# A cubic on VectorE factored so that GpSimd makes half of it, with a new order and more tiles on VectorE

## The chip, the cores and the metric

The kernel runs on one core of a Trainium2 chip. The metric is the device time of one execution in microseconds (us). The engines that matter here are TensorE (PE, with its weight loads PEld), ScalarE (ACT), VectorE (DVE) and GpSimd (POOL); transfers are issued from SyncE's queue (SP).

## The reference

Four layers in a row, with the weights of set A, B, A, B; each adds attention to the layer's input x of 2048 rows of 512, in float32:

```python
def _A_ref(x, wq, wk, wv, wo):          # _B_ref is the same
    B, S, D = x.shape                   # 1, 2048, 512
    H = 32
    Dh = D // H                         # 16
    q = (lambda x, *d: x.transpose(*d))((x @ wq).reshape(B, S, H, Dh), 0, 2, 1, 3)
    k = x @ wk
    v = x @ wv
    scores = jnp.einsum("bhqd,bkd->bhqk", q, k) * (Dh ** -0.5)
    p = _softmax(scores, axis=-1)
    o = jnp.einsum("bhqk,bkd->bhqd", p, v)
    return (lambda x, *d: x.transpose(*d))(o, 0, 2, 1, 3).reshape(B, S, H * Dh) @ wo
...
x = A_x
x = x + _A_ref(_layernorm(x, axis=-1), A_wq, A_wk, A_wv, A_wo)
x = x + _B_ref(_layernorm(x, axis=-1), B_wq, B_wk, B_wv, B_wo)
...                                     # A and B once more
```

One key head and one value head serve all 32 query heads. The scores are 4 layers x 32 heads x 2048 x 2048, which makes 4096 tiles of 128 partitions x 1024 columns, and every one of these numbers has to go through an exponential.

## The kernel before

The work is a sequence of pairs (layer, block of 512 queries, group of heads). For a score tile TensorE multiplies 64 keys by the queries (operands `kop` and `qt`), an engine takes the exponential into a slot of `pt` in SBUF (16 slots of 128x1024 float32, `NPT`), and TensorE multiplies that by the values (`vop`) into the accumulators `acc`.

There are two ways to the exponential. Most tiles go to one of two PSUM buffers `st` and ScalarE takes their exponential in one instruction (`score`, L813, letter S of the order). The others, 440 of the 4096, go in two halves through one PSUM bank, `by_v`, and VectorE makes the exponential itself (`exp_first` and the chain that it adds): two instructions of 512 columns scale the scores out of PSUM so that their integer bits are an exponent and a fraction (L845, letter I), and five instructions over the 1024 columns in SBUF then finish the tile: the fraction as a number between 1 and 2 (`mant`, L859), the power of two (L861), and a cubic in `mant` by Horner's rule, in three instructions that each have two inputs in SBUF (L862, L863 and L856). A tile's chain has two scratch buffers, `mant` and `poly`, and there are two sets of them, so that at most two chains are under way; the letters 0 and 1 of the order take the next instruction of the older and the younger one.

Beside this, TensorE makes the next layer's queries, keys and values and the last layer's output rows in the bank `beside`; VectorE empties that bank, sums and divides (letters X, G, D), and a one-column copy `seen` (L941, letter Y) lets it tell TensorE how far it may count. GpSimd squares the queries and keys for a range check (`sq` L476, `ksq` L452) and raises the variances to the power -1/2 (`rstd` L412).

What sets the order is a string written out in the program, `ORDER`: one letter for each step, and each engine's queue is filled in that order. Nothing is reordered later; each engine takes its own queue in order and waits for semaphores. A tile for VectorE is taken 24 half tiles ahead of ScalarE's (`AHEAD`).

Of the kernel before, what the change touches and what calls it, by code (L numbers as in the profile page):

```python
# [50 lines left out]
C0, C1, C2 = 7.247527122497559, 6.331161975860596, 0.5959731936454773  # L51
# [11 lines left out]
    "0SFSXaaXSsqGqS0qclSqIlqqSGlqqqrSYlmId0pSpml0Smp0ppmSppm0pSddpS0aaSQlmYeSXmlSXmalXSXFXSlmXaXXXSXgGpSGpmdI"
    "pSppmrYSqIcl0qSql0mSql0qeSqlm0SqalS0malSolSQmYppmpSppmdSXalXSmlmpSppmSsYGclIqSoqGrSIem0rSqlq0qSqe0lmSlmI"
    "Slm0aSpm0ppSpsmppISb0dSQlXmlS0maXSa0lqSql0qqSqlqlq0SqrmlSmGqqSIclSYmpppsSpGppImS0ppmpS0pmd0pSalS0mlmSQlX"
    "mlSXma0SqelqSoeSqlqqlqSrYmpSpmppIpsSIbm0prSd0bSGlS0lmaSGpmSIma0lSslmSIe0mlSQqlmXSa0aSXlm0SF0SlmlXXmS0iqS"
    "elIoS0qclSoqGSqrXaXSlXmIaSGlSXbb0S0pmppSQXpmXlmS0pmlSpmXdlXSmXlSalmSrdSXImaXlSXaS0lmcSGqloSGoqS0qelsSYIm"
    "ap0Sb0pSmp0pdSQpml0SddpSDDa0aSdlSYqqlmlXSslXmSeIeqSqrlqSqqlqqI0Sqa0lGSmqSDlmlqGSlSDDlma0SppmpSQ0dppmSpm0"
    "ppSddpXSlmlXSmaDDpSgYqqSqlqIrqSqIcl0Smr0lmSl0mSpmpIlmSGpslSGbdISa0aSslm1lSQ0qqlSqql0mlSImaS0alSDpmpmDpSD"
    "pdrSDDmlImlXSslS1maXlGSFXSaSGbd0SalS1ma0Sqelq0SqqlqSqeDlqDqSDcSIlma0SaS0bbSpmDDrpSIdd0pSgXmlSXmlS0qa0lqS"  # L70
    "qqlq0SqlmlSIqlqqS0lmaSYrpImpSpm0ppsSbIml0Spm0pSmal0SdlSd0aSrmlISpm0lsSm0al0SaSlqIme0SqlmSXalSXma0pSpdpSD"
    "mppDpmSDrmlISmg0lSqIqcS0c0eSrqqlqISql0mSfa1Sa0lSpmlm0Sp0mlSbImpSQa0lSml0sSqlmlSXmlImSgXlm0SqcISl0qqlq0So"
    "eSGmfS0alSIpmppSGpn1mS0pmprSma0l0SpmlSmIlpm0SpmlSm0apSsaIlSm0lsSlImql0Sqql0mSalXSmlXmrSIlmS0rFSXmaSDDp0d"
    "lSpm0lmSIpmlXSpmbSalSXXm0lmS0qelqS0qqlqSc0lqSscSIlmXlmS0rmlISpm0dpS0lmkSdIlS0mllsSm1aS0lmlSm0aSIa0lSrqml"
    "ISmg0Salm1Slm0SlmaIS0arS0mlmSlImlS0faS0aaSQlImS0asl0SmlImSg1lmGSmSGllS0maS1lm0lSmaSXalSm0aSlmXSIalm0SrmS"
    "ImaXlSmlS0rmlSXmaS0lSIlmmXSlsSIlmXmlSXrmlSmlXSlmmSlSXXmal0S1PPS0PP0SPPP0SPPS0PPSPS0aXa0SppmpSpmIdp0Sppsp"
    "mSIppmpS0salS0ma0Sc0eSoeISc0lqSqqreISmlXrmS1cl1qSql1mSqlml0SqlmS0aeSqIemS0lmlsSImlS0ppmg0SpmIbS0pbSpm0pm"
    "pSQprmSIlm0aSsa0SqeIeS0mlSXXlmXmrSIlmgX0SlmSXmaSGlGSXm1lS0almS0lmSlmXmlS0mlSX0malSImlSXlmDmlSXDmlXDSa0lm"
    "SrmlISmgXS1FXSXalmDDXSlmXSF0SlmXaSXlmSXXF0SXalmXSlm0SFISaXaSXlmS0PPPS0PPPSfDlSIma0SrlmDSDPPPDDS0PPIPSXml"
    "SXmal0SFSXmaXlXSmlXsSXXlXmXIeS0qqerSma1l1SolS0malSIqlqq0Saa0SaSpmp0pdSsppdISppmDkS0pmplmDDSQlmSIa0aS0qlq"  # L80
    "qSaXlSmXaS0pmpppSb0dSpmlSYqqrqeSIlq0mrSGloqlGSmmS0cIlSm0aSlm0lSmnpsSDDpmIa0SsalS0mlSIqa0rSIqlmlXSrmXaS0a"
    "eSq1qloS0elmS1qaS0lmeSIqcS0aaS0lmSppm0ppmSppsdISppm0psSpmIlmS0lmp0SlmmrSIlml1SqrmXlSmXaS0clqS1qce0SqqlSI"
    "mal0SmlS0pmpbSppmDpS0ddpSdDlDsSpmlImS0glmISa0rSqIqlqS0salSXma1lSmXaS0FSXmlSQ0qclqS0qlm0SlqmlS0meSqcIlS0m"
    "aSlqYrmSIpdp0pSrm0dpS0dnSmlGlSppmGSIpma0lSgSImlm1lSrm1qlSXmaS1lqqe0SolqSa0aSaISpm0nspSbImpS0lmrS0ma0lSqq"
    "eSIlm0eSqlqsSDDlIma0SlmS0dpsp0pSpmXaSa0eSolImSc0lSma0SlmrSIpmpd0pSsl0mpSIpmdp0SlmlS0mlmSqe0eSqlorISmeS0f"
    "a0SaIlSm0ppmpSdXlSml0qeSqc0SqalDSqeYsSlImb0Sppm0pSmp0pdSsa0lSQpmdSIal0SrmlmISlq0qqrSqa0lSIma0SlslmISppm0"
    "SlmfSGllSGmmSXXaDlSDmlmXSlm1lSXm1aSXa1lSmlmXS0lmlSXma0SalSXIma0SlmlSDDsIlmSmgXlS0maXISl0mrSXImal0SrmlS1m"
    "aXS1al0SFSXmlXSlmXaXSF0SlSXaXaSXXFISlmXSXaa0SFSXslmSIlmXlsS0mppmpSp1bS0bmpSp0bmS0lmlS0malSqqlIqS0qeqrScI"
    "eS0qiSIemXlSmXar0SFISmgXl0SmlmSQXlXmlSmX0aSlmXlXSX0maSlImlSX0maGSrSIgGlS0maDSlDmlDSml0mSlmlS1ma0Slml0Sml"
# [180 lines left out]
def fast_path(ctx, tc, x_in, weights, out, flag):  # L270
# [26 lines left out]
    def masks():  # L297
# [4 lines left out]
        with nc.allow_low_precision("zeros and ones"):  # L302
# [1090 lines left out]
```

## Time and profile before

| | |
|---|---|
| median of 3 runs | 3446.65 us (3446.0 to 3450.4) |
| the profiled execution | 3446.91 us, its span 3445.1 us |
| busy, share of the span: PE | 3371.2 us, 98% |
| ACT | 3389.2 us, 98%, 3686 instructions |
| DVE | 3267.9 us, 95%, 4420 instructions |
| POOL | 133.5 us, 4%, 137 instructions |
| granted TensorE clock | 0.998 |

The busy time of PE is modelled from pipelined matmuls; that of ACT and DVE comes from their own records. A DVE record begins a little before its predecessor's ends, so that the step from one start to the next tells more of what an instruction takes of the engine than its duration does.

### The profile page before, as it was taken

The page shows a single profiled execution, that of the slowest core. Times are in us where ns is not written, and L with a number is a line of the kernel's source. Part 1 is how long each engine was busy: PE and PEld are TensorE (multiplying, and loading weights), DVE is VectorE, ACT ScalarE, POOL GpSimd, SP SyncE. Part 2 cuts the span into 40 slices and gives each one's busy share as a digit, 9 for nine tenths or more (in the row PEclk, how much of TensorE's full clock was granted, in tenths as well). Part 3 has the DMA queues.
Part 4 walks back from the last instruction along what each step waited for, and adds up shares of the span by engine and source line. Part 5 has one row for each costly group of instructions (what it writes and reads, how often), then busy time and mean ns, then how long its engine had stood idle before and what let it go on. Part 6 is the DMA issues. An engine that isn't in the chain of part 4 may idle for free.

```text
span 3445.1 us, 206723 instructions
## 1 busy us (share of the span) xinstructions
PE 3371.2 (98%) x97983; PEld 2102.8 (61%) x97983; DVE 3267.9 (95%) x4420; ACT 3389.2 (98%) x3686; POOL 133.5 (4%) x137
## 2 busy tenths in 40 slices
PE   9999999999999999999999999999999999999998
PEld 5666666555566666656566666665656666565554
DVE  7889999999989999999998999999999899999998
ACT  8999999999999999999999999999999999999998
POOL 3000000000000000000000000000000000000000
PEclk9999999999999999999999999999999999999999
DMA  3221111010012111101002211110101211110010
GB/s 102 69 80 46 35 46 49 25 44 26 27 47 65 44 44 43 40 25 50 19 30 58 54 53 37 38 50 15 50 19 50 59 41 37 39 49 26 27 38 21
DMA packets 93826, 147.81 MB, mean 43 GB/s; under 512 B 30056, under 2 KB 47976, under 8 KB 92968
## 3 DMA queue, kind: packets, MB, share of 16 engines
q1 hardware_dynamic: 91400, 133.64, 13.2%
q8 instruction: 767, 12.57, 1.5%
q10 hardware_dynamic: 1568, 0.85, 0.1%
q14 instruction: 91, 0.75, 0.1%
HBM read 90.57 MB, written 34.59 MB: 36 GB/s over the span
## 4 chain that ended last, share of the span: by engine, by line
PE 58%; ACT 28%; DVE 8%; issue 2%; DMA 1%; SPq 0%; DVEq 0%; ACTq 0%
PE acc L531 31%; ACT pt L813 28%; PE st L531 15%; PE beside L531 9%; PE by_v L531 2%; DVE pt L845 1%; DVE poly L862 1%; DVE poly L863 1%; PE beside L425 1%; DVE pt L856 1%; DVE mant L859 1%; PE beside L568 1%; DMA qt<-qs 1%; DVE pt L861 1%; DMA rec<-rs 0%
## 5 line engine op out<-in xcount | busy, mean ns | idle before, releaser
L813 ACT ACTIVATE pt<-st 128x1024 f32<-128x1024 f32 x3656 | 3374.9, 1083 | 28.5 <-PE st L531 23.8
L531 PE MATMUL acc<-pt,vop 64*32 64x256 f32 (+1 forms) x52088 | 2904.6, 432 | 5.3 <-issue 2.0
L531 PE MATMUL st<-qt,kop 64*32 64x512 f16 x29248 | 1784.8, 380 | 44.4 <-ACT pt L813 28.9
L531 PEld LDWEIGHTS acc<-pt,vop 64*32 64x32 f32 x52088 | 1341.9, 106 | 273.5 <-DVE sum L960 15.0
L531 PEld LDWEIGHTS <-kop 64*32 64x32 f16 x32768 | 799.2, 90 | 904.4 <-issue 620.0
L845 DVE TENSOR_SCALAR pt<-by_v 128x512 int32<-128x512 f32 x880 | 601.8, 684 | 54.7 <-PE by_v L531 40.1
L863 DVE SCALAR_TENSOR_TENSOR poly<-poly,mant 128x1024 f32<-128x1024 f32 x440 | 538.7, 1225 | 3.8
L856 DVE SCALAR_TENSOR_TENSOR pt<-poly,pt 128x1024 f32<-128x1024 f32 x440 | 537.3, 1222 | 4.0
L862 DVE SCALAR_TENSOR_TENSOR poly<-mant 128x1024 f32<-128x1024 f32 x440 | 537.4, 1222 | 0.0
L531 PE MATMUL beside<-xnT,wq 64*32 64x512 f16 x5760 | 432.0, 376 | 1.0 <-DVE qs L480 0.4
L531 PE MATMUL beside<-wo,ot 64*32 64x512 f16 x5376 | 390.4, 376 | 1.2 <-DVE xt L500 1.1
L531 PE MATMUL by_v<-qt,kop 64*32 64x512 f16 x3520 | 352.3, 378 | 7.9 <-DVE pt L845 4.6
L859 DVE TENSOR_SCALAR mant<-pt 128x1024 int32<-128x1024 int32 x440 | 302.1, 687 | 13.6
L861 DVE TENSOR_SCALAR pt<-pt 128x1024 int32<-128x1024 int32 x440 | 303.6, 690 | 3.7
L531 PEld LDWEIGHTS <-wq 64*32 64x32 f16 x5760 | 167.7, 92 | 46.6 <-issue 10.5
L531 PEld LDWEIGHTS <-ot 64*32 64x32 f16 x5376 | 153.9, 92 | 40.7 <-issue 5.2
L476 POOL TENSOR_TENSOR sq<-qs 128x512 bf16<-128x512 f16 x64 | 75.4, 1178 | 885.1 <-DVE qs L473 867.9
L531 PE MATMUL beside<-xnT,wkv 64*32 64x512 f16 x1344 | 97.1, 376 | 1.2 <-issue 1.2
L960 DVE COPY sum<-acc 128x512 f32<-128x512 f32 x126 | 83.8, 685 | 8.9 <-PE acc L531 6.3
L412 POOL TENSOR_TENSOR rstd<-var,nhalf 128x4 f32<-128x4 f32 x15 | 23.5, 1566 | 1428.7 <-DVE var L411 1428.7
L473 DVE TENSOR_SCALAR qs<-beside 128x512 f16<-128x512 f32 x62 | 42.4, 684 | 11.2 <-PE beside L531 4.6
L500 DVE SCALAR_TENSOR_TENSOR xt<-beside,xt 128x512 f32<-128x512 f32 x61 | 42.0, 688 | 6.1 <-PE beside L531 4.0
(124 smaller groups left out, 802.6 us busy)
## 6 DMA issues: line engine op xcount, KB each, us to landing
qt<-qs SPq DMA_DIRECT2D x85, 512.0 KB
qs<-qs SPq DMA_DIRECT2D x127, 128.0 KB
rec<-rs SPq DMA_DIRECT2D x63, 256.0 KB
xs<-xt SPq DMA_DIRECT2D x48, 256.0 KB
xt<-xs SPq DMA_DIRECT2D x48, 256.0 KB
sum<-sum SPq DMA_DIRECT2D x252, 32.0 KB
xt<-in_A_x_dram SPq DMA_DIRECT2D x30, 256.0 KB
out_dram<-xt SPq DMA_DIRECT2D x15, 256.0 KB
```

Of the source, the lines that this page charges most:

```text
L473: V.tensor_scalar(qs[:, 0], ps, BIG, -BIG, ALU.min, ALU.max)
L476: G.tensor_tensor(sq, qs[:, 0], qs[:, 0], ALU.mult)
L500: V.scalar_tensor_tensor(x, ps, 1 / VS / WS, x, ALU.mult, ALU.add)
L531: PE.matmul(o[32 * j:32 * j + 32], w[j][h], x[j][h], start=start, stop=stop, skip_group_check=True, tile_position=(64 * r, 32 * j))
L813: e = A.activation(pts[:, i], st[s], AF.Exp, scale=SCALE / UP / UP).ins
L845: w = V.tensor_scalar(e[:, 512 * r:512 * r + 512], by_v, SCALE / UP / UP * LOG2E * 2.0 ** 23, LEAD, ALU.mult, ALU.add).ins
L856: writer[i] = V.scalar_tensor_tensor(p, poly, C0, p, ALU.add, ALU.mult).ins
L859: lambda: V.tensor_scalar(mant.bitcast(I32), e, 0x3FFFFF, 0x3F800000, ALU.bitwise_and, ALU.bitwise_or),
L861: lambda: V.tensor_scalar(e, e, 0x7FC00000, HALVES, ALU.bitwise_and, ALU.bitwise_or),
L862: lambda: V.scalar_tensor_tensor(poly, mant, C2, mant, ALU.add, ALU.mult),
L863: lambda: V.scalar_tensor_tensor(poly, poly, C1, mant, ALU.add, ALU.mult),
L960: V.tensor_copy(sums[pr, odd], acc[odd])
```

## The change

The cubic is written as (m + r)(m(m + b) + c), with r `ROOT`, b `SLOPE` and c `REST`. Right behind the write of `mant`, GpSimd makes `poly` in two instructions over 128x1024 float32 in SBUF: m + b (b read from a 128x1 tile, broadcast along the row), and that times m. VectorE keeps two of its three instructions of the cubic, p = (m + r) p, which needs nothing from GpSimd, and p = (poly + c) p, which waits for GpSimd's second. The order string is replaced by another, with 508 tiles on VectorE and 3588 on ScalarE (before 440 and 3656).

```diff
-C0, C1, C2 = 7.247527122497559, 6.331161975860596, 0.5959731936454773
+ROOT, SLOPE, REST = 1.0617902024664836, -0.4658170088210063, 6.825761911968984
...
+    slope = one.tile([P, 1], F32, name="slope")
+    V.memset(slope, SLOPE)
...
+        def first():
+            V.tensor_scalar(mant.bitcast(I32), e, 0x3FFFFF, 0x3F800000, ALU.bitwise_and,
+                            ALU.bitwise_or)
+            G.tensor_tensor(poly, mant, slope.to_broadcast([P, 1024]), ALU.add)
+            G.tensor_tensor(poly, poly, mant, ALU.mult)
+
         def last():
-            writer[i] = V.scalar_tensor_tensor(p, poly, C0, p, ALU.add, ALU.mult).ins
+            writer[i] = V.scalar_tensor_tensor(p, poly, REST, p, ALU.add, ALU.mult).ins
 
         chains.append(deque([
-            lambda: V.tensor_scalar(mant.bitcast(I32), e, 0x3FFFFF, 0x3F800000, ALU.bitwise_and,
-                                    ALU.bitwise_or),
+            first,
             lambda: V.tensor_scalar(e, e, 0x7FC00000, HALVES, ALU.bitwise_and, ALU.bitwise_or),
-            lambda: V.scalar_tensor_tensor(poly, mant, C2, mant, ALU.add, ALU.mult),
-            lambda: V.scalar_tensor_tensor(poly, poly, C1, mant, ALU.add, ALU.mult),
+            lambda: V.scalar_tensor_tensor(p, mant, ROOT, p, ALU.add, ALU.mult),
             last]))
```

In the order string the letters for TensorE's steps around S are other too; 62 letters Y (`seen`) become 229, and 84 letters P (a product over the whole array at once) become 60, the rest being done in steps of the half arrays. The letters X, D, F, G and Q are as many as before.

In VectorE's queue, some four tenths of the way through, the tiles stand one behind another before (`pt<-by_v` are the two halves of a tile, `mant` opens the chain, and `pt<-poly` closes it; the numbers tell buffers apart):

```order
L845 TENSOR_SCALAR pt<-by_v 128x512
L859 TENSOR_SCALAR mant_38253<-pt 128x1024
L861 TENSOR_SCALAR pt<-pt 128x1024
L862 SCALAR_TENSOR_TENSOR poly_38254<-mant_38253 128x1024
L845 TENSOR_SCALAR pt<-by_v 128x512
L863 SCALAR_TENSOR_TENSOR poly_38254<-poly_38254,mant_38253 128x1024
L845 TENSOR_SCALAR pt<-by_v 128x512
L856 SCALAR_TENSOR_TENSOR pt<-poly_38254,pt 128x1024
L859 TENSOR_SCALAR mant_38378<-pt 128x1024
```

In the changed queue the lines have moved (L847 the halves, L858 `mant`, L868 the power of two, L869 the factor m + r, L864 the closing product):

```order
L847 TENSOR_SCALAR pt<-by_v 128x512
L858 TENSOR_SCALAR mant_39159<-pt 128x1024
L864 SCALAR_TENSOR_TENSOR pt<-poly_39043,pt 128x1024
L868 TENSOR_SCALAR pt<-pt 128x1024
L847 TENSOR_SCALAR pt<-by_v 128x512
L869 SCALAR_TENSOR_TENSOR pt<-mant_39159,pt 128x1024
L847 TENSOR_SCALAR pt<-by_v 128x512
L858 TENSOR_SCALAR mant_39264<-pt 128x1024
L864 SCALAR_TENSOR_TENSOR pt<-poly_39160,pt 128x1024
```

A tile is closed behind the opening of the next one now, one Horner instruction is gone, and between `mant` and the closing product of a tile stands a whole period of the queue.

GpSimd's queue before, in the first layer, holds the range check and the variances alone:

```order
L412 TENSOR_TENSOR rstd<-var,nhalf 128x4
L452 TENSOR_TENSOR ksq<-kop_2_99 128x512
L412 TENSOR_TENSOR rstd<-var,nhalf 128x4
L452 TENSOR_TENSOR ksq<-kop_3_100 128x512
L476 TENSOR_TENSOR sq<-qs 128x512 x12
```

In the changed kernel, at the same place (L454 `ksq`, L478 `sq`):

```order
L860 TENSOR_TENSOR poly_2978<-mant_2977,slope 128x1024
L861 TENSOR_TENSOR poly_2978<-poly_2978,mant_2977 128x1024
L454 TENSOR_TENSOR ksq<-kop_3_102 128x512
L860 TENSOR_TENSOR poly_3300<-mant_3299,slope 128x1024
L861 TENSOR_TENSOR poly_3300<-poly_3300,mant_3299 128x1024
L478 TENSOR_TENSOR sq<-qs 128x512
L860 TENSOR_TENSOR poly_3683<-mant_3682,slope 128x1024
L861 TENSOR_TENSOR poly_3683<-poly_3683,mant_3682 128x1024
```

The pairs `poly` (1016 instructions in all) have come between the others.

More of the change, by code (lines that the diff above doesn't have):

```diff
@@ L63 @@
[L63 to L77, printed above, removed]
@@ L228 @@
[L228 to L230 removed]
+    "QXPPPPPPPPSSPPPPSXlXmSPPSPPSPPPPSrSPPPPSIsXlmSIaXaS0lmS0F0SaaXSlmXSaXXaSQXlmXSlmXXlmSXaX0SalSGSXaXgSGFIS"
+    "XlmrSXmaXlSIFS0lmXSaXaSXXF0SXmalXSml0SQFSXaaXSlm0qSqleSYGmdnSsIpmnSpmlSYGrqqlIqqSqel0qS0mlqS0lmeSmaYpSpm"
@@ new lines @@
+    "ppSmplXmSlmXSQXlmXmlXSFSXXaX0aSaXaXXSmSGfXlISGlslSImaXrSXaXSXlmXmSXaX0lSm0mSIlmlXsSXFISaXSQXlmaXS1F1SaXS"
+    "aXlmSXXFGSfXlSGlS0aaXSlm0SFSXlmlImSXlmS0bbS0pspmpSQbIpSmYe0lqS0qlo0ScqlSqqlqqSgYIlmSpdGrSmIlmgXSXlmSGFlS"
+    "0maSXlXmlSXmlmXS0aXlXSXXmXaSQ0lmXlISmXlmS0alSmXGfSIaXaSXsSGlmXaXXS0mSaIlmXSrmSXF0SXaa0SXalmXS0FSQaXSlmXl"
+    "mXXSF0SaXSaXaSGFGSlSIlmXfSXae0SqlIoS0lqql0qSqseSIqclSmY1pd1Sppmp0SQbdp0SpmnSmXalXSmlXSXmlXFSrmXXlXSXXmIa"
+    "pGSpppSGps0pmpSppmIpmSppmYl0Sqqc0Sc0eSqcSqlqXlmSQaXSlmdpSp0mppSmpppmSppmpSmkYlqSIlqqlqSqqrqlSqIqeS0lq0ml"
@@ new lines @@
+    "SGmmSGelSXmaXSlm0pSdpb0SQpmnSpmdpSYlmlqSqqlqSlqqlqqSrqlqSqqIlYmSpmlSXaXlsSImpppmS0pmp0dSpGlS0nmaSGpmppSm"
+    "YelqSQqqeS0lqqeSqYlmSqYalqSqlmSlmgSXXImaSrIFSXXma0Spp0mppSpm0aSppmlSYXqGqlqSGmmSXeXlqXqSQe0mSqlmlSYXbXmp"
+    "SdXlXSmaXlSmlSrqqlmXSIqegSmYplSIXma0SaXlSGoqqS0lqmGlSoeS0lmaSQYppmSppmpmS0ppmlSYqqlmSYpYmeSqglSYbImpSdXl"
+    "SmaXrSIceSmY0lS0pmbGSlpSGpmd0pSalSQYmppmSY0clqSqlqDDqSqlqlYmSppmpSYmeXrSmalISmXgSeImlSY0bd0Sdl0SmllSGnSD"
+    "pmGdpSDaDlSQ0mlmpSpmDDlYSqqYalSqqlqSqYlmlSqrmlSYIpmgYSqlImlqS0mg0SaIaGSrqqSIaXaSGllS0maS1lmlXSQmg1Sm0alS"
@@ new lines @@
+    "FISXma0rSppmpSIpmppm0rSpmlS0pmIaSDpmlS0pmlGSpspmDlGSmSDmaIlSq0qeSeq1jSa0aSqlIqSlm0a0SlqqsSlImlm1Slqq1Slm"
+    "XaSXrmlmS0ppmpSpImplm0SppspmSIpml0SsalSImd0pSa0lS0mlmrSqlIoS1qcl1Smrql1SmaSa0lSmlImSDDpslYmISqe1eSf1aS0q"
+    "lqSaXaXSaSIpmp0pkSmppmIpSd0lSsa0lSbImS0a0lSmlmSDqlqeDSDqrqlqISml0qSfaSIe0lmS0lmqSQ0lqmlSslImSc1lmS1lmrS1"
+    "malSd0dSlmlXSmXlmSGpmpIpSpppGsSIppmp0mSglmISppm0pSm0al0SmlSroIlqqSqc1lS1mrql1SmalS0qlmSlmIlqSDDqlsqSIaXa"
+    "S1lmSXa1gSm0aSFISXmar0SalSImaXrSmlSmalS1a0SlmlmXXS0lmSIa0aSlsmISlmXls1Sma0SalSDmlDmlDSmlS0bIbSXpmdpSp0bS"
@@ new lines @@
+    "pmpmXrSlImlS0faS0qc0Sqlq0lqSqqeSXqeeSmIaSXlsIlmSlr0mSlmISQlm0lsSImlm0Ssa0lSmlDDS1maSGmlXSmlSGla0Sa0SaIaX"
+    "SrmlISml0mrSa1Sa0aSmSIlm0lsSImlm0rSmlS1alm0SmSIaXaSsSIlmXaSsaSlmSXXmal1Sqql0qS0qlqqSlo0qlSqqqSIlm0mrSIlm"
+    "S0fnmp1Sppm0pSpmppm0SnmIpSmlXa0SppmpSpsIpmpSps0bSppmIpSm0al0Sml0SqrqloSIqllq1qSrq1eqSlq1mlSqlmXSlm0aSpbI"
+    "SpmDpspSIbmSY1eqql0sSqel0qSqlIoSe0orSQaIaSY1gd0SpmlSIpmdlXXSmlDSDalmXS0rmlSXImaXSslGlSXGmmS0alSm1aSXlm1l"
+    "SmX0aSaIlSmXlm0SlmlSXm0arSlmISXg0mlISml0mSlXmrXSFISXgml1SmXaSXF0SmlXSlmXlmSXXF0SmlSXaIaSXlmrS0FISXmgS1aX"
@@ new lines @@
+    "aS1loS0qlqqlqS1qlqqSc0lqSmaISl0mrSppmIbS0ppspmS0ppmpS0mnmlSXmlSXmaXlSIFSXmaXlXSXmXlXXS0lqqqjSIqel0qSflIq"
+    "Sqql0qS0aaSgDDmISQpdnS1rm1aS0apSdIaS0lspmSpmIlmSY1glm0SpmnSmIal0SlSGqlDmSGmfDlDSmlISmg0lSml1mpSXaS1aXaS1"
+    "lmqSql0qeSqqlqISqe0lqSqflIqSa0Smr0lmSpIpmn0SpmppsSImlm1pSsa1lSb0mSal0SdlmSIpmlXSrmXaSlIqqe0SqqrlqS0qcIlS"
+    "m0aS0lmlSspmInSb1dS1lspm0SalSdId0SalSDDflYmSIqlqq1lSs0lmSa0aS0bpSmaXlSXmaSIe0eSrqqqlISqlq0mrSa0qlS0meSQq"
+    "eDlqSDmaIlSDmlsDDSpIpmppm0SrpmpS0bdISppm0gSIpmlSXml1mSgGlSGmmS1a0lSmaS1alSXma0SFSDlmDaDSlmSXlmIaS0qlqjSq"
@@ L231 @@
+    "SraIS0lsmSIlm0lsSlm1Sa0aSlm0SaIa0SlmSfaSalSmIS110aaS0SaaSmSal0malmal"
 )
```

303 lines of the change are left out of this document (145 added, 158 removed).

## The prediction

> **What bounds the kernel now.** I read the page's busy times first, then the groups of instructions, then the waits, and last the time order of VectorE and GpSimd at single places.
>
> ```profile
> PE 3371.2 (98%) x97983; PEld 2102.8 (61%) x97983; DVE 3267.9 (95%) x4420; ACT 3389.2 (98%) x3686; POOL 133.5 (4%) x137
> ...
> L813 ACT ACTIVATE pt<-st 128x1024 f32<-128x1024 f32 x3656 | 3374.9, 1083 | 28.5 <-PE st L531 23.8
> ...
> L845 DVE TENSOR_SCALAR pt<-by_v 128x512 int32<-128x512 f32 x880 | 601.8, 684 | 54.7 <-PE by_v L531 40.1
> L863 DVE SCALAR_TENSOR_TENSOR poly<-poly,mant 128x1024 f32<-128x1024 f32 x440 | 538.7, 1225 | 3.8
> L856 DVE SCALAR_TENSOR_TENSOR pt<-poly,pt 128x1024 f32<-128x1024 f32 x440 | 537.3, 1222 | 4.0
> L862 DVE SCALAR_TENSOR_TENSOR poly<-mant 128x1024 f32<-128x1024 f32 x440 | 537.4, 1222 | 0.0
> ...
> L859 DVE TENSOR_SCALAR mant<-pt 128x1024 int32<-128x1024 int32 x440 | 302.1, 687 | 13.6
> L861 DVE TENSOR_SCALAR pt<-pt 128x1024 int32<-128x1024 int32 x440 | 303.6, 690 | 3.7
> ```
>
> ScalarE is the bound: its exponentials fill 3374.9 us of a span of 3445.1, 3374.9 / 3656 = 0.923 us for each, and it stands idle for only 28.5 us ahead of them. VectorE follows closely with 3267.9 us, and GpSimd has next to nothing to do. The waits say the same, from both sides:
>
> ```profile
> PE st L531 <- ACT pt L813: 28.9, 84, 0.5
> ACT pt L813 <- PE st L531: 23.8, 42, 5.6
> ```
>
> TensorE waits for ScalarE about as long as the other way round, both hardly at all. So a tile moved off ScalarE is worth 0.923 us as long as VectorE keeps up. Whether it does is the whole question.
>
> **What VectorE saves.** The price of an instruction is the step from its start to the next one's, in a stretch where nothing waits:
>
> ```profile
> 611.94 0.68 DVE L861 TENSOR_SCALAR pt<-pt 128x1024 int32<-128x1024 int32 x1
> 612.54 1.22 DVE L862 SCALAR_TENSOR_TENSOR poly<-mant 128x1024 f32<-128x1024 f32 x1
> 613.79 1.22 DVE L863 SCALAR_TENSOR_TENSOR poly<-poly,mant 128x1024 f32<-128x1024 f32 x1
> 614.93 0.68 DVE L845 TENSOR_SCALAR pt<-by_v 128x512 int32<-128x512 f32 x1
> 615.53 1.21 DVE L856 SCALAR_TENSOR_TENSOR pt<-poly,pt 128x1024 f32<-128x1024 f32 x1
> ```
>
> That is 0.60 us for a scaling out of PSUM (614.93 to 615.53), 0.60 for an integer instruction in SBUF (611.94 to 612.54), and 1.14 for a Horner instruction (613.79 to 614.93). A tile costs VectorE 2 x 0.60 + 2 x 0.60 + 3 x 1.14 = 5.82 us before and 4.68 after. 440 x 5.82 = 2561 us leaves 3267.9 - 2561 = 707 us for all its other work, which is moved but not changed. The letters Y rise by 167, at 0.15 us (the mean below): 25 us. So without anything else VectorE would be busy for 707 + 508 x 4.68 + 25 = 3109 us, 158 us less than now, though it has 68 tiles more.
>
> ```profile
> L941 DVE COPY seen<-beside 128x1 f32<-128x1 f32 x62 | 9.3, 150 | 22.7 <-PE beside L531 20.0 <-PE st L531 2.0
> ```
>
> ScalarE saves 68 x 0.923 = 63 us. TensorE's products are the same in number (a score of a VectorE tile goes to `by_v` and not to `st`), and no transfer is added. Those edits are costed at nothing.
>
> **What GpSimd costs.** The trace of before has no GpSimd instruction of 128x1024. Its nearest rows are these, in the preparation, where nothing holds them up:
>
> ```profile
> 14.27 1.75 POOL L1114 TENSOR_TENSOR wq<-pt,wq 128x128 f16<-128x128 f32 x4
> ...
> 18.80 1.47 POOL L1114 TENSOR_TENSOR wq<-pt,wq 128x256 f16<-128x256 f32 x2
> ...
> 24.77 1.45 POOL L1114 TENSOR_TENSOR wq<-pt,wq 128x256 f16<-128x256 f32 x2
> ```
>
> One takes 1.75 / 4 = 0.44 us over 128 columns and 2.92 / 4 = 0.73 over 256: 0.29 for 128 columns more, 0.15 fixed, so 0.44 + 7 x 0.29 = 2.47 us over 1024. The squares below, with 16-bit inputs, take 1.04 over 512, so 0.15 + 2 x 0.89 = 1.93. I take 2.3, nearer to the first, which has a float32 input; the ends are 1.9 and 2.5. GpSimd's 1016 instructions then fill 2337 us: it has room for them in its own queue. By the Trainium skill, GPSIMD Engine Reference, section 3.1, an elementwise addition of two float32 tensors over 2048 columns takes 4497 ns there, so an estimate by it is 2.25 us; the sum below would be 1016 x 0.05 = 51 us lower by it. No run shown here has that shape.
>
> What decides is what the two engines do to one another. Three places, each a GpSimd `sq` with the VectorE instructions beside it, behind the row of all of them (shortest, median and longest):
>
> ```profile
> L476 POOL TENSOR_TENSOR sq<-qs x64: 1040/1042/1954, 17.8 to 2879.8; 128x512 bf16<-128x512 f16 x64
> ```
>
> ```profile
> 1101.88 1.04 POOL L476 TENSOR_TENSOR sq<-qs 128x512 bf16<-128x512 f16 x1 [11.14 <-DVE qs L473]
> ```
>
> ```profile
> 1101.84 0.69 DVE L480 TENSOR_TENSOR qs<-beside,qs 128x512 f16<-128x512 f32 x1
> 1102.44 1.56 DVE L856 SCALAR_TENSOR_TENSOR pt<-poly,pt 128x1024 f32<-128x1024 f32 x1
> ```
>
> ```profile
> 1073.08 1.04 POOL L476 TENSOR_TENSOR sq<-qs 128x512 bf16<-128x512 f16 x1 [18.74 <-DVE qs L473]
> ```
>
> ```profile
> 1073.64 1.02 DVE L861 TENSOR_SCALAR pt<-pt 128x1024 int32<-128x1024 int32 x1
> ```
>
> ```profile
> 1116.78 1.21 DVE L863 SCALAR_TENSOR_TENSOR poly<-poly,mant 128x1024 f32<-128x1024 f32 x1
> ```
>
> ```profile
> 1116.94 1.95 POOL L476 TENSOR_TENSOR sq<-qs 128x512 bf16<-128x512 f16 x1 [14.01 <-DVE qs L473]
> ```
>
> An `sq` takes 1.04 us. A Horner instruction that starts while one runs takes 1.56 us and not 1.22; an integer instruction in SBUF takes 1.02 and not 0.69. An `sq` that finds a Horner instruction running takes 1.95. The instruction with one input in PSUM (L480) keeps its 0.69 in the middle of an `sq`. So the two engines exclude each other wherever VectorE works in SBUF alone, in both directions, and the later one waits.
>
> The price: L856 ended at 1104.00, 1.22 of work behind 1102.78, which is 0.14 ahead of the end of `sq`. And the blocked `sq` ended at 1118.89, 0.90 behind L863's end at 1117.99. In alternation, the end of one VectorE instruction to the end of the next is 0.90 - 0.14 + 1.22 = 1.98 where it is 1.14 without `sq`: GpSimd's 1.04 us cost VectorE 0.84, its duration less 0.20. At 2.3 us that is 2.10 (1.70 and 2.30 at the ends). By the Trainium skill, SBUF — State Buffer, section Who interferes with whom, the shared pair of ports is a lock held for the whole instruction, and the other engine blocks fully. The rows agree that it blocks; held to the recorded end it would cost 0.14 more each, and the sum below 142 us more, but the rows show it let go 0.14 us early, and I go by them.
>
> Now the changed queue, at the place shown with the change. Behind `mant` VectorE goes on at once with the closing product of the tile before, and GpSimd's addition waits for it like the `sq` at 1116.94. Then the addition runs and L868 waits for it; then GpSimd's product runs and L869 waits for that, with a scaling out of PSUM (L847) beside it that is not held up. Of a tile's six instructions on VectorE four work in SBUF alone, 0.60 + 0.60 + 1.14 + 1.14 = 3.48 us; with 2 x 2.10 for GpSimd that is 7.68 us of a port that only one has at a time, against 3445 / 508 = 6.8 us for a tile in the present time.
>
> The gross cost is 1016 x 2.10 = 2134 us. What comes off is VectorE's work with PSUM that happens to stand where it waits anyway. The scalings are 1016 x 0.60 = 610 us. Of the other 707 us these four groups are in SBUF alone, 147 us of records, 127 us in steps:
>
> ```profile
> L1005 DVE TENSOR_TENSOR ot<-sum,ot 128x512 f16<-128x512 f32 x63 | 43.5, 691 | 1.8
> ...
> L1008 DVE TENSOR_TENSOR sum<-sum,rec 128x512 f32<-128x512 f32 x63 | 43.0, 683 | 4.8 <-DMA rec<-rs 3.4 <-issue 1.3
> ...
> L419 DVE TENSOR_SCALAR xn<-xt,mv,rstd 128x512 f32<-128x512 f32 x64 | 34.0, 542 | 1.6 <-POOL rstd L412 1.5
> L1002 DVE CAST ot<-sum 128x512 f16<-128x512 f32 x63 | 26.5, 421 | 0.8
> ```
>
> That leaves 610 + 707 - 127 + 25 = 1215 us that collide with nothing. I went through the changed VectorE queue from each `mant` to the next and added up what of this stands in the two gaps where GpSimd has the port (behind the first and the second SBUF instruction that follows `mant`, or straight behind `mant` where such work comes first): 43%, so 522 us. The rest stands where GpSimd has nothing to do, since a tile's pair is done by then and the next `mant` is still to come.
>
> **The sum.** 3109 + 2134 - 522 = 4721 us of VectorE, busy or blocked. Of its present idle time, 3445.1 - 3267.9 = 177 us (start, end, and waits for TensorE), I keep the same 57% as of the uncovered work, 101 us: 4822. The profiled execution took 3446.91 us, 1.8 more than its span, and stands 0.3 above the median; with that, 4824, told as 4825 us. VectorE becomes the bound, and TensorE and ScalarE wait for its tiles. GpSimd's `rstd`, below, now stands in a queue behind up to two such instructions, 15 times at most 4.6 us, 69 us, and `xn` waits for it on VectorE; I cost it at nothing, since VectorE is blocked in that time anyway, and leave it to the upper end.
>
> ```profile
> L412 POOL TENSOR_TENSOR rstd<-var,nhalf 128x4 f32<-128x4 f32 x15 | 23.5, 1566 | 1428.7 <-DVE var L411 1428.7
> ```
>
> **The rivals.**
>
> First, the port is busy all the time: all of the 1215 us find a place beside GpSimd, since a blocked VectorE lets TensorE get ahead, so that its scalings never wait. 3109 + 2134 - 1215 = 4028, with some 40 us at both ends about 4070; from 3660 to 4270 for 1.9 to 2.5 us. For it speaks that GpSimd takes its turn between two VectorE instructions; against it that the order is fixed and puts work behind L869 where GpSimd is out of work.
>
> Second, the engines fall into step on top of it: a late VectorE frees `by_v` late, TensorE takes its queue in order, and VectorE then waits for each tile's scores.
>
> ```profile
> DVE pt L845 <- PE by_v L531: 40.1, 70, 3.0
> ```
>
> Such a wait is 40.1 / 70 = 0.57 us now; one for each of 508 tiles adds 290 us, 5115. TensorE's slack speaks against it, since a slower VectorE gives it time to be early.
>
> Third, on the other side: the collisions hardly happen, because the two engines pass the port back and forth within an instruction over float32, or because waits fall into VectorE's idle time. Then ScalarE sets the time, 3447 - 63 = 3384 us. It decides where an average GpSimd instruction costs VectorE no more than 158 / 1016 = 0.16 us, for then VectorE is as busy as now. The smallest collision above cost 0.33. Between 0.16 and about 0.7 us the time would be from 3450 to 3950.
>
> **How the numbers follow.** The forecast case, 4400 to 5050 by the bounds of GpSimd's duration (1.70 and 2.30 give 4417 and 5027), has 0.56. The busy port (3950 to 4400) has 0.20, the engines in step (above 5050) 0.13, weak collisions (3450 to 3950) 0.06. Faster, by weak collisions under 0.16 us, has 0.04, and 0.01 is left for within 0.2%, about what a measurement of this kernel can tell from no change. Slower is 0.95. The range from 4100 to 5150 leaves out the three small cases beyond it and the outer parts of the rivals, 2 in 10 together.
>
> **What would show it.** In the changed profile the records of L868 and L869 should be 1 to 2.5 us longer on average than 0.69 and 1.22, while the scalings (L847) stay at 0.68; GpSimd should be busy well over 60% of the span with 2.3 us or more for an instruction; ScalarE's share should fall to about 70% with waits for TensorE's scores, and TensorE should wait for VectorE's tiles. Horner instructions still at 1.22 us would refute the step on the port. A GpSimd instruction under 1.9 us without a VectorE instruction beside it would refute its size. The prediction is wrong if VectorE's blocked time is much less than 1600 us.

## The result, and the profile after

The changed kernel takes 4864.15 us (median of 4 runs, 4860.6 to 4865.49) against 3446.32 us before: a ratio of 1.4109, 95% interval 1.4085 to 1.4134. It is slower by 1418 us; 4825 us had been forecast. Of the executions of the kernels below one was slow, 4146.73 us at a granted clock of 0.752 (the kernel with a quadratic), and its times leave that one out.

From the profile's page of the changed kernel, the busy times, TensorE's granted clock over the span in 40 slices, and the costliest groups:

```profile
PE 3777.5 (78%) x97759; PEld 2251.1 (46%) x97759; DVE 4564.7 (94%) x4556; ACT 3448.0 (71%) x3618; POOL 2825.2 (58%) x1153
...
PEclk9998999998999899989889999999999998888898
...
L815 ACT ACTIVATE pt<-st 128x1024 f32<-128x1024 f32 x3588 | 3433.8, 1035 | 1382.8 <-PE st L533 1315.3
...
L860 POOL TENSOR_TENSOR poly<-mant,slope 128x1024 f32<-128x1024 f32 x508 | 1231.2, 2424 | 1676.2 <-DVE mant L858 1676.1
...
L861 POOL TENSOR_TENSOR poly<-poly,mant 128x1024 f32<-128x1024 f32 x508 | 1455.3, 2865 | 39.8
L869 DVE SCALAR_TENSOR_TENSOR pt<-mant,pt 128x1024 f32<-128x1024 f32 x508 | 1219.3, 2401 | 3.7
...
L864 DVE SCALAR_TENSOR_TENSOR pt<-poly,pt 128x1024 f32<-128x1024 f32 x508 | 855.1, 1683 | 10.4 <-POOL poly L861 7.9
L847 DVE TENSOR_SCALAR pt<-by_v 128x512 int32<-128x512 f32 x1016 | 690.5, 680 | 88.1 <-PE by_v L533 57.3
L868 DVE TENSOR_SCALAR pt<-pt 128x1024 int32<-128x1024 int32 x508 | 759.7, 1496 | 5.8
```

ScalarE has dropped from 98% to 71% and stands idle for 1382.8 us in front of exponentials, nearly all of it for TensorE's scores. VectorE is the engine that is full, and not with more instructions but with longer ones: the factor m + r (L869) records 2.40 us on average where a Horner instruction took 1.22, the power of two (L868) 1.50 where it took 0.69, the closing product (L864) 1.68. The scalings out of PSUM (L847) stand at 0.68 us as before.

From the list of waits of the changed kernel (who waited for whom: us in total, times, longest):

```profile
POOL poly L860 <- DVE mant L858: 1676.1, 488, 17.3
...
ACT pt L815 <- PE st L533: 1315.3, 880, 7.6
PE by_v L533 <- DVE pt L847: 739.5, 426, 7.5
```

This is the route by which the loss gets to ScalarE: VectorE empties `by_v` late, TensorE waits there 426 times with its queue behind it, and the scores for ScalarE come late. GpSimd waits for VectorE far more than the other way round: it is idle for 1676 us until the next `mant`, and VectorE's closing product waited for GpSimd's result only 7.9 us in all (the row of L864 above).

One tile in the order of time, from the VectorE and GpSimd rows of the changed kernel's timeline (start, us, instruction):

```profile
1821.76 0.68 DVE L858 TENSOR_SCALAR mant<-pt 128x1024 int32<-128x1024 int32 x1
1822.36 1.21 DVE L864 SCALAR_TENSOR_TENSOR pt<-poly,pt 128x1024 f32<-128x1024 f32 x1
1823.50 2.38 DVE L868 TENSOR_SCALAR pt<-pt 128x1024 int32<-128x1024 int32 x1
1825.80 0.68 DVE L847 TENSOR_SCALAR pt<-by_v 128x512 int32<-128x512 f32 x1
1826.40 2.79 DVE L869 SCALAR_TENSOR_TENSOR pt<-mant,pt 128x1024 f32<-128x1024 f32 x1
```

```profile
1822.52 2.81 POOL L860 TENSOR_TENSOR poly<-mant,slope 128x1024 f32<-128x1024 f32 x1 [1.77 <-DVE mant L858]
1825.41 2.70 POOL L861 TENSOR_TENSOR poly<-poly,mant 128x1024 f32<-128x1024 f32 x1
```

It is the walk of the prediction, step for step. L864 has the port and GpSimd's addition waits for it; L868 waits for the addition and the product (L861) for L868; L869 waits for the product, while L847, which reads PSUM, goes through at 0.68 us in the middle of it.

### The profile page after: what moved, and what is told of

It reads as the page before. It is cut to its first block, busy times and chain, and to the rows that moved or that the text cites. A ratio compares the mean times of both kernels' runs of the same rounds, so it can differ in the third digit from the quotient of the medians.

```text
span 4863.7 us, 207696 instructions
## 1 busy us (share of the span) xinstructions
PE 3777.5 (78%) x97759; PEld 2251.1 (46%) x97759; DVE 4564.7 (94%) x4556; ACT 3448.0 (71%) x3618; POOL 2825.2 (58%) x1153
## 4 chain that ended last, share of the span: by engine, by line
DVE 71%; PE 16%; issue 10%; ACT 1%; DMA 1%; POOL 0%; SPq 0%; DVEq 0%
DVE pt L869 17%; DVE pt L868 13%; DVE pt L864 13%; DVE pt L847 10%; PE acc L533 7%; DVE mant L858 7%; PE st L533 4%; PE beside L533 3%; DVE sum L1014 2%; PE by_v L533 1%; ACT pt L815 1%; DVE ot L1011 1%; DVE xn L421 1%; DVE ot L1008 1%; DVE sum L966 1%
## 5 line engine op out<-in xcount | busy, mean ns | idle before, releaser
L815 ACT ACTIVATE pt<-st 128x1024 f32<-128x1024 f32 x3588 | 3433.8, 1035 | 1382.8 <-PE st L533 1315.3
L533 PE MATMUL acc<-pt,vop 64*32 64x256 f32 (+1 forms) x51696 | 3255.7, 467 | 73.2 <-DVE sum L966 51.0
L860 POOL TENSOR_TENSOR poly<-mant,slope 128x1024 f32<-128x1024 f32 x508 | 1231.2, 2424 | 1676.2 <-DVE mant L858 1676.1
L533 PE MATMUL st<-qt,kop 64*32 64x512 f16 x28704 | 2142.3, 406 | 13.1 <-ACT pt L815 8.7
L533 PEld LDWEIGHTS acc<-pt,vop 64*32 64x32 f32 x51696 | 1467.1, 112 | 499.0 <-issue 104.8
L861 POOL TENSOR_TENSOR poly<-poly,mant 128x1024 f32<-128x1024 f32 x508 | 1455.3, 2865 | 39.8
L869 DVE SCALAR_TENSOR_TENSOR pt<-mant,pt 128x1024 f32<-128x1024 f32 x508 | 1219.3, 2401 | 3.7
L533 PE MATMUL by_v<-qt,kop 64*32 64x512 f16 x4064 | 448.4, 418 | 749.2 <-DVE pt L847 739.5
L864 DVE SCALAR_TENSOR_TENSOR pt<-poly,pt 128x1024 f32<-128x1024 f32 x508 | 855.1, 1683 | 10.4 <-POOL poly L861 7.9
L847 DVE TENSOR_SCALAR pt<-by_v 128x512 int32<-128x512 f32 x1016 | 690.5, 680 | 88.1 <-PE by_v L533 57.3
L868 DVE TENSOR_SCALAR pt<-pt 128x1024 int32<-128x1024 int32 x508 | 759.7, 1496 | 5.8
L858 DVE TENSOR_SCALAR mant<-pt 128x1024 int32<-128x1024 int32 x508 | 415.6, 818 | 18.5 <-ACT pt L815 0.5
L478 POOL TENSOR_TENSOR sq<-qs 128x512 bf16<-128x512 f16 x64 | 83.0, 1298 | 176.5 <-DVE qs L475 176.5
L947 DVE COPY seen<-beside 128x1 f32<-128x1 f32 x229 | 33.9, 148 | 70.7 <-PE beside L533 59.5
```

What stands on the lines that cost most here:

```text
L478: G.tensor_tensor(sq, qs[:, 0], qs[:, 0], ALU.mult)
L533: PE.matmul(o[32 * j:32 * j + 32], w[j][h], x[j][h], start=start, stop=stop, skip_group_check=True, tile_position=(64 * r, 32 * j))
L815: e = A.activation(pts[:, i], st[s], AF.Exp, scale=SCALE / UP / UP).ins
L847: w = V.tensor_scalar(e[:, 512 * r:512 * r + 512], by_v, SCALE / UP / UP * LOG2E * 2.0 ** 23, LEAD, ALU.mult, ALU.add).ins
L858: V.tensor_scalar(mant.bitcast(I32), e, 0x3FFFFF, 0x3F800000, ALU.bitwise_and, ALU.bitwise_or)
L860: G.tensor_tensor(poly, mant, slope.to_broadcast([P, 1024]), ALU.add)
```

## The experiments

The theory (called the port theory in the expectations): GpSimd and VectorE exclude each other wherever VectorE works in SBUF alone, and the turns that VectorE waits are the whole loss. The rivals: that VectorE waits for GpSimd's results (late results), and that the new order itself loses the time (order theory). Times before, on the same chip as the first four, 3444.42 us, and as the last four, 3443.61 us.

**The new order without GpSimd's help** (`e1_all_vector`):

```diff
-            G.tensor_tensor(poly, mant, slope.to_broadcast([P, 1024]), ALU.add)
-            G.tensor_tensor(poly, poly, mant, ALU.mult)
+            V.scalar_tensor_tensor(poly, mant, SLOPE, mant, ALU.add, ALU.mult)
```

> The new order with its 508 tiles, but VectorE makes m(m + b) itself where GpSimd did, in a third Horner instruction; GpSimd is back to the range check and the variances. Port theory (GpSimd and VectorE exclude each other in SBUF, and that alone makes the changed kernel slow): VectorE is busy 707 + 25 + 508 x 5.82 = 3689 us and bounds, 3750 to 3900 us, and no Horner instruction is longer than 1.25 us on average. Late results (VectorE waits for GpSimd's product): the same, since nothing is waited for. Order theory (the new order itself, with 229 touches, loses the time): 4500 us or more, for VectorE has still more to do than in the changed kernel.

Measured: 3927.73 us, a ratio of 1.1402 (1.138 to 1.1425), a little above the range. Its busy times:

```profile
PE 3468.8 (88%) x97759; PEld 2097.7 (53%) x97759; DVE 3704.7 (94%) x5064; ACT 3421.0 (87%) x3618; POOL 128.0 (3%) x137
```

VectorE has 508 more Horner instructions than in the changed kernel and is busy 860 us less. The 3704.7 us are the 3689 of the sum; the range was missed because the idle time was set too low (220 us, with a span of 3924.6). The order is not what costs 1418 us.

**The pair left out** (`e2_no_pair`; the two lines of GpSimd are dropped, and `poly` is two tiles filled once with 0.5):

> The changed kernel without GpSimd's pair: m(m + b) is left out, and the closing product reads two tiles that are filled once at the start. Everything else, the order too, stays. Port theory: VectorE is busy 3109 us, ScalarE bounds, 3384 to 3420 us, which is 1 to 2% faster than before. Order theory: the time stays far above before, 4000 us or more. Late results: like the port theory, 3384 to 3420 us; this run does not tell those two apart.

Measured: 3395.08 us, 0.9859 (0.9843 to 0.9876), faster than before. The busy times and the exponentials of this kernel:

```profile
PE 3333.3 (98%) x97759; PEld 2118.3 (62%) x97759; DVE 3117.1 (92%) x4556; ACT 3332.7 (98%) x3618; POOL 130.3 (4%) x139
```

```profile
L818 ACT ACTIVATE pt<-st 128x1024 f32<-128x1024 f32 x3588 | 3318.5, 1077 | 33.5 <-PE st L536 26.1 <-PE beside L536 1.6
```

VectorE's 3117.1 us are near the 3109 of the prediction, and ScalarE stands at 98% again. TensorE does too, and no run separates the two as the bound. So the order with 508 tiles does bring most of the 68 tiles' worth of 63 us, 49 by the medians, if GpSimd is silent. Against this kernel GpSimd's pair costs (4864 - 3395) / 508 = 2.89 us for a tile; VectorE's own Horner instruction, in the run above, (3928 - 3395) / 508 = 1.05 us.

**GpSimd work that nobody waits for** (`e3_idle_pair`), added to the kernel before:

```diff
+    alone = one.tile([P, 192], F32, name="alone")
+    G.memset(alone, 1.0)
...
+            for _ in range(7):              # behind each mant
+                G.tensor_tensor(alone, alone, alone, ALU.mult)
```

> The kernel before, with its old order and its cubic, to which GpSimd work is added that nobody waits for: behind each mant GpSimd multiplies a small tile of its own, 128x192 float32, by itself seven times, about 0.57 us each, 3080 instructions, about 4 us for a tile, as the pair. Port theory: each instruction of VectorE that works in SBUF alone finds GpSimd busy and waits for some 0.37 us (0.57 less 0.20); of about 2450 of them most are hit, so VectorE loses 550 to 800 us beyond its slack, 4000 to 4250 us in all, with the scalings out of PSUM still at 0.68 us. Late results: 3440 to 3460 us, since no result is used. Order theory: 3440 to 3460 us, since the order is the old one.

Measured: 3899.28 us, 1.132 (1.1297 to 1.1343), 100 us under the range of the port theory and far from 3460. From its groups:

```profile
L864 POOL TENSOR_TENSOR alone<-alone 128x192 f32<-128x192 f32 x3080 | 2744.3, 891 | 234.4
L869 DVE SCALAR_TENSOR_TENSOR poly<-mant 128x1024 f32<-128x1024 f32 x440 | 635.7, 1445 | 0.0
...
L847 DVE TENSOR_SCALAR pt<-by_v 128x512 int32<-128x512 f32 x880 | 596.7, 678 | 39.0 <-PE by_v L533 30.0 <-PE st L533 8.2
L868 DVE TENSOR_SCALAR pt<-pt 128x1024 int32<-128x1024 int32 x440 | 392.8, 893 | 3.7
```

The order is the old one and no result is used, yet Horner instructions grow from 1.22 to 1.45 us and integer ones from 0.69 to 0.89, while the scalings do not. This ends both rivals as the main cause. The estimate was too high for another reason than the number of hits. The rows of single records (shortest, median, longest in ns):

```profile
L869 DVE SCALAR_TENSOR_TENSOR poly<-mant x440: 1187/1507/1926, 41.2 to 3872.5; 128x1024 f32<-128x1024 f32 x147
```

```profile
L864 POOL TENSOR_TENSOR alone<-alone x3080: 498/833/4330, 37.1 to 3801.3; 128x192 f32<-128x192 f32 x193
```

More than half of the Horner records stand 0.29 us or more above 1.22, so most are hit, as was expected. But a hit costs about 0.3 us and not 0.37: GpSimd's multiplication takes 0.50 us undisturbed where 0.57 was taken, and 0.50 - 0.20 is 0.30.

**Memsets in place of the pair** (`e4_memset`; `for _ in range(4): G.memset(poly, 0.5)`, m(m + b) left out):

> The changed kernel with GpSimd's pair replaced by four memsets of the same poly tile, about 1.0 us each by the step of the 128x256 memsets at the start (0.26), 4.2 us for a tile as the pair; m(m + b) is left out, and the closing product waits for the last memset as it did for the product. Port theory, if any use of SBUF by GpSimd shuts VectorE out: 4500 to 4900 us. Late results: the product is as late as in the changed kernel, 4700 to 4900 us. Port theory, if only what GpSimd reads collides with a second input of VectorE: Horner instructions stay at 1.22 us, and the time is 3400 to 3800 us. By the Trainium skill, SBUF — State Buffer, section Who interferes with whom, a two-input instruction collides with a GpSimd instruction that reads, not with one that only writes, and an integer instruction in its two-port mode collides with both; so L868 would be longer and L869 not.

Measured: 3665.66 us, 1.0642 (1.062 to 1.0663). From its groups:

```profile
L861 POOL MEMSET poly<- 128x1024 f32 x2032 | 2248.5, 1109 | 657.8 <-DVE pt L864 568.9 <-DVE seen L947 1.2
...
L864 DVE SCALAR_TENSOR_TENSOR pt<-poly,pt 128x1024 f32<-128x1024 f32 x508 | 619.3, 1219 | 3.5 <-POOL poly L861 0.8 <-DVE seen L947 0.3
L869 DVE SCALAR_TENSOR_TENSOR pt<-mant,pt 128x1024 f32<-128x1024 f32 x508 | 617.0, 1215 | 3.7
L868 DVE TENSOR_SCALAR pt<-pt 128x1024 int32<-128x1024 int32 x508 | 505.4, 995 | 5.8
```

GpSimd records 2249 us of memsets here, not much less than the pair's 2687, and the Horner instructions stand at 1.22 us as if it were silent. Of a tile's instructions only the integer ones grow, L868 to 1.00 us. So what collides with an instruction of two SBUF inputs is GpSimd's reading; an integer instruction with one input also collides with GpSimd's writing. That is the rule that the expectation takes from the Trainium skill, SBUF — State Buffer, section Who interferes with whom, and this run agrees with it. The time lies in the range given for it, and far under the 4500 us and more that late results, or a collision with any use of SBUF, would have made.

**The prices by themselves** (`e5_prices`, a kernel that computes no attention):

> The disputed prices by themselves: no attention at all, the output is left at zero. VectorE runs twelve instructions of one kind, first a Horner instruction, then an integer instruction in SBUF, a scaling out of PSUM and a row statistic with one SBUF input; beside each, GpSimd runs nothing, or twelve of one kind: a product of two float32 tiles, a sum with a broadcast column, a product of a tile with itself, the same over 512 columns of 16 bits, a sum with a constant (one input), a memset. Port theory: Horner and integer instructions take turns with everything that reads two inputs, so that their steps grow from 1.14 and 0.60 us by GpSimd's duration less 0.20; scalings and statistics keep 0.60 us beside all of them; beside memsets the Horner instruction keeps 1.14 and the integer one waits. GpSimd alone: 2.36 us for two tiles, 1.89 with the broadcast column, about 1.0 for the memset. If the engines instead shared the port's rate, the steps beside GpSimd would all be longer by the same share, scalings included.

From the timeline of its one execution, twelve instructions in each row: VectorE's first, in the order of the text below, then GpSimd's beside the scalings.

```profile
11.17 13.70 DVE L82 SCALAR_TENSOR_TENSOR vo<-va,vb 128x1024 f32<-128x1024 f32 x12
25.49 37.29 DVE L82 SCALAR_TENSOR_TENSOR vo<-va,vb 128x1024 f32<-128x1024 f32 x12
65.53 32.37 DVE L82 SCALAR_TENSOR_TENSOR vo<-va,vb 128x1024 f32<-128x1024 f32 x12
135.27 22.98 DVE L82 SCALAR_TENSOR_TENSOR vo<-va,vb 128x1024 f32<-128x1024 f32 x12
159.70 18.74 DVE L82 SCALAR_TENSOR_TENSOR vo<-va,vb 128x1024 f32<-128x1024 f32 x12
196.05 13.71 DVE L82 SCALAR_TENSOR_TENSOR vo<-va,vb 128x1024 f32<-128x1024 f32 x12
210.29 7.31 DVE L85 TENSOR_SCALAR vo<-va 128x1024 int32<-128x1024 int32 x12
218.21 30.89 DVE L85 TENSOR_SCALAR vo<-va 128x1024 int32<-128x1024 int32 x12
326.77 13.14 DVE L85 TENSOR_SCALAR vo<-va 128x1024 int32<-128x1024 int32 x12
363.23 18.01 DVE L85 TENSOR_SCALAR vo<-va 128x1024 int32<-128x1024 int32 x12
381.78 7.25 DVE L89 TENSOR_SCALAR vo<-ps 128x512 f32<-128x512 f32 x12
389.64 7.25 DVE L89 TENSOR_SCALAR vo<-ps 128x512 f32<-128x512 f32 x12
```

```profile
389.74 27.62 POOL L95 TENSOR_TENSOR gz<-gx,gy 128x1024 f32<-128x1024 f32 x12
418.00 22.24 POOL L98 TENSOR_TENSOR gz<-gx,gs 128x1024 f32<-128x1024 f32 x12
476.79 32.85 POOL L107 TENSOR_SCALAR gz<-gx 128x1024 f32<-128x1024 f32 x12
```

Twelve Horner instructions take 13.70 us alone, 37.29 beside products of two tiles, 32.37 beside sums with a broadcast column, 22.98 beside squares over 512 columns of 16 bits, 18.74 beside sums with a constant, 13.71 beside memsets. Beside the first three, which are two-input instructions, eleven of the twelve wait a turn, so a turn costs (37.29 - 13.70) / 11 = 2.14 us, (32.37 - 13.70) / 11 = 1.70 and (22.98 - 13.70) / 11 = 0.84; the last is the price that the prediction read at `sq`. Undisturbed, beside scalings out of PSUM, GpSimd takes 27.62 / 12 = 2.30 and 22.24 / 12 = 1.85 us from one start to the next. Twelve integer instructions go from 7.31 to 30.89 us beside products, 2.14 a turn; twelve scalings take 7.25 us with and without, and twelve row statistics with one SBUF input 7.21 us with and without. Beside GpSimd's two-input instructions it is strict turn-taking and no sharing of a rate.

The sum with a constant (L107), GpSimd's instruction with one input, does not fit that. Undisturbed it takes 32.85 / 12 = 2.74 us, longer than the others, but VectorE gets two Horner instructions through beside each of them: only six of the twelve start within the 18.74 us. So one costs VectorE (18.74 - 13.70) / 6 = 0.84 us there. Beside integer instructions it is more: four start within the 13.14 us, (13.14 - 7.31) / 4 = 1.46 us each.

**A small dose** (`e6_every_eighth`), in the old order with 440 tiles: VectorE makes m(m + b) in a Horner instruction, but for every eighth tile GpSimd's pair does.

```diff
+            if helped:                      # tile number % 8 == 0, right behind mant
+                G.tensor_tensor(poly, mant, slope.to_broadcast([P, 1024]), ALU.add)
+                G.tensor_tensor(poly, poly, mant, ALU.mult)
...
+            if not helped:
+                V.scalar_tensor_tensor(poly, mant, SLOPE, mant, ALU.add, ALU.mult)
```

> The kernel before, with its old order and 440 tiles, the cubic factored as in the change; GpSimd makes m(m + b) for every eighth tile on VectorE, 55 in all, and VectorE makes it itself for the others in a Horner instruction. Port theory: for a helped tile VectorE saves 1.14 us and loses some 3 us, 55 x 1.9 = 105 us, part of it in its present idle time: 3450 to 3520 us, no dose pays. Late results: VectorE is busy 63 us less, and the product has a Horner instruction's time to come: 3430 to 3450 us.

Measured: 3557.5 us, 1.0327 (1.0309 to 1.0344), above the port theory's range and farther still from the other. Its busy times:

```profile
PE 3400.5 (96%) x97983; PEld 2109.8 (59%) x97983; DVE 3345.2 (94%) x4366; ACT 3399.4 (96%) x3686; POOL 418.0 (12%) x247
```

55 helped tiles cost 114 us, 2.07 us each. VectorE is busy 77 us more than before, under the 105 worked out, but its idle time rose too, from 177 to 213 us: the slack on VectorE did not absorb anything. Of these 36 us 17 are waits for GpSimd's result, so late results have a small share here, where in the old order a tile is closed before the next one is opened:

```profile
DVE pt L872 <- POOL poly L865: 17.0, 8, 2.3
```

This dose does not pay; others were not tried.

**The addition alone** (`e7_add_alone`; the line of GpSimd's product is dropped, and with it the factor m):

> The changed kernel with only the first of GpSimd's pair, poly = m + b; the product with m is left out. The closing product still waits for GpSimd, 2.4 us earlier. Port theory: the cost goes by the port's time, 508 x (1.89 - 0.20) = 858 us of the pair's 1956, and a little more than in proportion above the kernel without the pair, 3850 to 4100 us. Late results: the result is in time for nearly every tile, 3400 to 3600 us.

Measured: 3997.46 us, 1.1609 (1.1585 to 1.1632), as the port theory has it. From its groups:

```profile
L860 POOL TENSOR_TENSOR poly<-mant,slope 128x1024 f32<-128x1024 f32 x508 | 1205.7, 2374 | 2215.1 <-DVE mant L858 2214.9
L863 DVE SCALAR_TENSOR_TENSOR pt<-poly,pt 128x1024 f32<-128x1024 f32 x508 | 764.7, 1506 | 2.5
L868 DVE SCALAR_TENSOR_TENSOR pt<-mant,pt 128x1024 f32<-128x1024 f32 x508 | 737.6, 1453 | 3.7
L867 DVE TENSOR_SCALAR pt<-pt 128x1024 int32<-128x1024 int32 x508 | 730.5, 1438 | 5.8
```

The result is there long before it is used (the closing product, L863, lists no wait for it), and one instruction of GpSimd for a tile still costs (3997 - 3395) / 508 = 1.19 us. That is 602 us of the pair's 1469, 41%, where its share of the port's time is 858 / 1956 = 44%: a little less than in proportion, not more.

**A version that beats both** (`e8_quadratic`): the order with 508 tiles pays if a tile has two Horner instructions and GpSimd none, so the cubic is made a quadratic.

```diff
-LEAD = 1030161728.0
-ROOT, SLOPE, REST = 1.0617902024664836, -0.4658170088210063, 6.825761911968984
+LEAD = 1047889856.0
+SLOPE, REST = 0.4016341690549174, 2.106132903999927
...
-            G.tensor_tensor(poly, mant, slope.to_broadcast([P, 1024]), ALU.add)
-            G.tensor_tensor(poly, poly, mant, ALU.mult)
...
-            lambda: V.scalar_tensor_tensor(p, mant, ROOT, p, ALU.add, ALU.mult),
+            lambda: V.scalar_tensor_tensor(poly, mant, SLOPE, mant, ALU.add, ALU.mult),
```

> The changed kernel with a quadratic in place of the cubic: VectorE makes m(m + b) itself, and the factor m + r is dropped, so that a tile still has two Horner instructions and GpSimd none. The quadratic is off by at most 2.2e-4 of the exponential over the half octave, the cubic by 4.8e-6 (both worked out from the coefficients). Port theory: like the kernel without the pair, 3385 to 3415 us, faster than before and than the change. Order theory: 4000 us or more. If the Horner instruction behind the integer one waits for mant's end, VectorE has slack for it (its idle time without the pair is some 270 us).

Measured: 3394.01 us, 0.9849 (0.9829 to 0.9869) of the kernel before, and in the range. It buys 1.5% with some 45 times the error of the cubic in an eighth of the exponentials.

## Why the prediction was right, point by point

**ScalarE's 63 us** are there for the most part, but only with GpSimd silent: 3445.1 - 3391.5 = 54 us of span in the run without the pair, where its exponentials fill 3318.5 us, 56 less than before.

**VectorE's 3109 us** without GpSimd measured 3117.1 (the same run), and 3109.8 in the quadratic kernel.

**The duration of GpSimd's instructions** was mis-sized: 2.3 us was taken for both. The rows of the two lines in the changed kernel (shortest, median, longest record in ns):

```profile
L860 POOL TENSOR_TENSOR poly<-mant,slope x508: 1887/2399/3003, 36.3 to 4833.9; 128x1024 f32<-128x1024 f32 x170
```

```profile
L861 POOL TENSOR_TENSOR poly<-poly,mant x508: 2356/2707/3415, 38.8 to 4836.4; 128x1024 f32<-128x1024 f32 x170
```

Unhindered (the shortest records) they take 1.89 and 2.36 us, 2.12 on average. By the Trainium skill, GPSIMD Engine Reference, section 3.1, an estimate was 2.25; the product, whose inputs are two tiles, is 0.11 above it, and the sum with a broadcast column 0.36 below.

**The turn costs the duration less 0.20 us**: 1.89 - 0.20 = 1.69 and 2.36 - 0.20 = 2.16, against the 1.70 and 2.14 of the prices. This step, read from single pairs of rows of before, held to 0.02 us. As a rule it is too wide in two places: not everything that VectorE does in SBUF alone is hit (the row statistics are not), and GpSimd's sum with a constant, 2.74 us, costs far less than its duration. Neither is in the pair. The gross cost is then 508 x (1.69 + 2.16) = 1956 us and not 2134.

**What hides in it**: VectorE is busy or blocked for 4564.7 us, 1448 more than without the pair, so by difference 1956 - 1448 = 508 us were hidden, against 522 counted from the order. `rstd`, costed at nothing, made VectorE wait for 0.7 us in all by the list of waits.

**The idle time** is the step that failed: 101 us were left to VectorE, and it has 4863.7 - 4564.7 = 299. That it would shrink in proportion was an argument without a row. In the old order, with GpSimd's work that nobody waits for, it did shrink, though not to 57%: 3898.4 - 3757.9 = 140 us. In the new order it is 220 us with all on VectorE and 3994.4 - 3784.2 = 210 with the addition alone, and 274 in the run without the pair, where VectorE is not the bound. So by these runs some 110 of the missing 198 us belong to the new order. Part of that is at its touches (`seen`), which the sum had at their own 0.15 us and at no wait: VectorE's waits there for `beside` were 20.0 us before. The other 80 or so come with the pair, and what makes them is not shown. In the changed kernel the two longest waits are those of the touches (L947) for `beside` and of the scalings for `by_v`:

```profile
DVE seen L947 <- PE beside L533: 59.5, 74, 2.6
DVE pt L847 <- PE by_v L533: 57.3, 81, 3.6
```

So two errors met: VectorE's total came out 156 us too high (4721 against 4564.7), 2134 - 1956 = 178 of it GpSimd's duration less 14 for what hides and 8 for VectorE's own work, and its idle time 198 us too low. The forecast missed by 39 us because they have opposite signs. That it came so near is luck; the price of a turn, which makes most of the loss, is not.

**The signs** named ahead hold in part. L869 is 1.18 us longer, the scalings stay at 0.68 and ScalarE falls to 71%, as was said. But L868 is 0.81 us longer where at least 1 was named, GpSimd is busy for 58% of the span and not well over 60%, and its addition, at 1.89 us, is just under the 1.9 that was to refute the size. VectorE's blocked time is 1448 us, less than 1600 but not much less.

**The rivals.** The port that is always busy did not happen: only 508 of some 1215 us found cover, by the difference above. The engines in step may be in the result in part, as extra idle time, but not as one wait for each tile: the scalings waited for `by_v` 81 times. Weak collisions are excluded by the prices. The bound at which the change would have decided itself, 0.16 us for a GpSimd instruction, stands against a measured 1448 / 1016 = 1.43 us net.

## What to carry to other kernels

An engine with 4% load is not free help: look in the trace for the places where it already runs, and compare the instructions beside it with their undisturbed length, shape by shape. Here three pairs of rows of before, at GpSimd's small `sq`, gave the price of a turn to 0.02 us and with it a forecast of +40% that the busy times alone would have called -2%. By the price kernel GpSimd can help beside VectorE's work on PSUM, or where it only writes and VectorE has two inputs; a schedule for it has to count turns and not utilization. The form of the instruction counts too: m + b as a sum with a constant would take GpSimd longer than the broadcast column (2.74 us against 1.85) and may cost VectorE less (0.84 to 1.46 us against 1.70). No run tried that in the attention.

## What the runs showed of the hardware that was not expected

Memsets back to back do not take turns: in the price kernel the first integer instruction waited for the whole row of twelve, 11.40 us, and the other eleven ran at full speed behind it.

```profile
363.23 11.40 DVE L85 TENSOR_SCALAR vo<-va 128x1024 int32<-128x1024 int32 x1
```

```profile
363.30 10.78 POOL L110 MEMSET gz<- 128x1024 f32 x12
```

A GpSimd instruction with one input, a sum of a tile with a constant, is the slowest of them over 1024 columns, 2.74 us undisturbed, and yet it cost VectorE's Horner instructions only 0.84 us each. And TensorE's granted clock, at 0.998 before, was 0.916 in the changed kernel and 0.988 to 1.0 in all the other attention kernels; TensorE was busy for 78% of the span there and 87% or more in the others. Whether the lower clock added to VectorE's waits, 299 us in all, was not tried; VectorE's scalings took 0.68 us at both clocks.
